# DeltaNet with an MLP: half of the batches with their token halves exchanged

## The chip, the cores and the metric

The kernel runs on one core of a Trainium2 chip. What is measured is the device time of one execution in microseconds (us), and what is compared is the median of several executions. One further execution is recorded by the hardware profiler; from it come the page of the profile and the trace.

A core has five engines that run side by side, each of them in its own program order: TensorE (PE in the profile) multiplies matrices, VectorE (DVE), ScalarE (ACT) and GpSimd (POOL) do elementwise work, and SyncE (SP) only issues transfers (DMAs). They meet at semaphores. PE's array of 128 by 128 can be used in smaller pieces, here called places: a matmul that contracts over at most 32 or 64 rows and writes 32 or 64 output partitions takes only the place at those rows and columns, and matmuls at other places can run beside it. The profile gives a place as rows*columns, `32*32` or `48*64` (48 rows lie in a place of 64).

## The reference

There are 4 batches of 8 heads, 768 tokens, and a head dimension of 48. Every (batch, head) pair carries a 48 by 48 state, and its tokens are a recurrence:

```python
k_n = k / (np.linalg.norm(k, axis=-1, keepdims=True) + 1e-06)
for t in range(S):
    y[:, :, t] = einsum('bhd,bhde->bhe', q_t, state)
    v_old = einsum('bhde,bhd->bhe', state, k_t)
    state = state + beta_t * einsum('bhd,bhe->bhde', k_t, v_t - v_old)
```

The heads of a token, side by side, make a row of 384 numbers. Of each row x the kernel then computes a LayerNorm without offset, two products with a ReLU between them (384 to 1536 and back to 384), and adds x: `x + relu(xn @ w_ch1) @ w_ch2`.

## The kernel before, in words

**Chunks.** The 768 tokens are 12 chunks of C = 64, and a chunk is two blocks of BK = 32 tokens. Within a chunk the recurrence is a triangular system. With the Gram matrix of the keys (the products of every pair of keys in the chunk) and the state S from the chunk before, a chunk needs these steps:

- `ks` = K S and `qs` = Q S, in `recur` (L886): what the old state answers to keys and queries. `ks` goes to the PSUM tile `two`, `qs` to the tile `by`. DVE then subtracts `ks` from v (L893).
- U, the solution of the triangular system, in three products (L908). The first multiplies v of one block by the inverse of that block's diagonal part (`xd`); ACT copies it to `u` (L914). The second multiplies it by the off-diagonal part of the Gram matrix (`goff`); DVE subtracts it from v of the other block (L912). The third multiplies that by the other block's inverse, and ACT copies again.
- the new state (L929, called s) and y = qs + P U (L919), where P holds the masked products of keys and queries (`pt`).

**Layout.** The 32 (batch, head) pairs are 2 pairs of batches (e) by 2 batches in a pair (g) by 8 heads; a head is j and a parity hp. A chunk of tokens of one pair of batches lies in one `half` of the partitions, 64 rows, and a block in one `quad`, 32 rows. The j index runs over 8 values, j = 0 to 3 for the batch g = 0 and j = 4 to 7 for g = 1. Each step loops over j and over the four (hp, e). In U a matmul reads 32 rows (a quad) and writes 32 partitions (a quad), and with (hp, e) alone the 64 matmuls of a product use four places.

**Gram.** For chunks up to 4, `gram` (L608 and what it calls) and `queries` (L643) make the Gram matrix and the key-query products apart. From chunk 5 on (JOINT), `gram_queries` (L666, its matmuls in L680) makes both: for each head and each of the two blocks one matmul at a place of 48*32, with 64 key columns and 64 query columns as moving data, 128 in all. For the second block the 32 columns that stand for the first block's tokens are not used afterwards. ACT copies the diagonal parts to `gdiag` (L691) and the off-diagonal ones to `goff`; DVE masks the key-query products into `pt`.

**Inverses.** `rows_inverse(m)` inverts the diagonal blocks of two chunks, 2m+1 and 2m+2, on DVE: a transposition of `gdiag` (L828), 31 pairs of row operations (L849, L856), and a transposition at the end (L861), which gives X(m) to U. Chunk 0 has a shorter way, `rows_near` and `near_join` (L807 to L819), and its U is called u0.

**Keys and queries.** `load_raw` and `load_v` load k and v with tokens on partitions (four DMAs and two DMAs for a chunk). `load_blocks` loads k or q once more in blocks, in eight DMAs, and `turned` (L577) transposes them on DVE; for chunks 0 to 3 PE transposes k instead (`first_kt`). The results stay in slots shared with other data: `kts`, `qts` and `pts` have four each, some in the same memory as the inverses' scratch tiles and `e_`, `d_` of the MLP.

**MLP.** The MLP of a chunk is 256 tokens. For chunks 0 to 2 the first product is plain (L1184, units of 6 matmuls); from chunk 3 on it is `fifteen` (L1100), 15 products of sub-blocks. The second product is plain for chunk 0 (L1206, pairs of matmuls), and `seven` (L1281), seven products in place of eight, from chunk 1 on. Sums and differences of sub-blocks are on GpSimd, DVE and ACT (L1267, L1113, L1306).

**Order.** `add` and `pe` only collect steps with what they read and write. `line.emit(ORDER)` then emits them as the list ORDER of step numbers has it, and `in_this_order` makes this each engine's program order, for DMA issues too. So the list alone decides where a small block of the recurrence stands between the matmuls of the MLP on PE. Before the first real work PE runs 26 steps of matmuls on zeros (`warm`, L1364), and three more (`fill`).

Of the kernel before, what the change touches and what calls it, by code (L numbers as in the profile page):

```python
# [16 lines left out]
C = 64  # L17
# [40 lines left out]
def pool(n):  # L58
# [161 lines left out]
def kernel(  # L220
# [16 lines left out]
    DM = H * D  # L237
    DFF = w_ch1.shape[1]
    KC = DM // 128
    FT = DFF // 128  # L240
    GH = 2 * H
    NP = H // 2
    TURNED = 4
    LNPE = 2
    GP = 2 * NP
    FROM = 3
    TOK = 256
    WN = 768

# [96 lines left out]
    def one_of(c):  # L346

        return c % 2 if c < 3 else (0, 0, 2, 3)[c - 3 if c < 4 else 1 + (c - 4) % 3]

    def kt_of(c):  # L350
        return c if c < 4 else (c - 4) % 3
# [513 lines left out]
    def xt_keys(c):  # L865
        return [("xd", slot(c))]
# [613 lines left out]
```

## Time and profile before

| | us |
|---|---|
| median of three runs | 512.43 (509.69 to 512.50) |
| the profiled execution | 510.23 |
| its span (first to last instruction) | 508.5 |
| granted clock, mean | 0.981 |
| PE busy | 486.6 (96% of the span) |
| DVE busy | 387.7 (76%) |
| POOL busy | 248.8 (49%) |
| ACT busy | 187.3 (37%) |
| L908, U products | x2304 matmuls of 0.201 each, many at a time |
| L680, joint Gram | x896 matmuls of 0.269 each |
| L886, ks and qs | x1344 matmuls of 0.218 each |
| issues on SP | 323 DMAs |

Busy time counts an engine as busy while any of its instructions runs, so it does not say how full PE's array is. In the lines of a timeline the columns are the start, the duration of the whole group in us, engine, source line, operation, output<-input, for a matmul the place and the tile, and the number of instructions. The duration of a group reaches to the end of its last instruction, which overlaps with the first of the next; what a block costs is read from one start to the next start. In the table of windows, each row is a stretch of the span, with the busy time of each engine and the number of its instructions (x), the clock granted to PE (1.00 is full), the share of time in which the DMA engines moved data, and GB/s.

### The profile page before, as it was taken

The numbers are of one execution on the slowest core, as the hardware profiler recorded it, in microseconds if no ns is written. First come the engines' busy times: TensorE is split into PE (matmuls) and PEld (weight loads), VectorE is DVE, ScalarE is ACT, GpSimd is POOL, SyncE is SP. The second block draws the span as 40 slices with busy tenths as digits, with TensorE's granted clock in tenths as the row PEclk, the third lists the DMA queues.
The fourth block names the chain that finished last, engine by engine and source line by source line (L and its number), as shares of the span: only waits on it lengthen the run. The fifth ranks groups of instructions, "written<-read, shape, count | busy, mean of one in ns | idle before, by whom it ended". The sixth has DMA issues, their size and how long they took to land.

```text
span 508.5 us, 21970 instructions
## 1 busy us (share of the span) xinstructions
PE 486.6 (96%) x9688; PEld 437.7 (86%) x9688; DVE 387.7 (76%) x855; ACT 187.3 (37%) x404; POOL 248.8 (49%) x377
## 2 busy tenths in 40 slices
PE   8668799999999999999999999999999999999996
PEld 5456686778898899999999989999999999999995
DVE  0865999989999967849999848999979889363241
ACT  2785544535512224442233433413431421424130
POOL 5036223302574588582291464492681671826553
PEclk9969799999999999999999999999999999999999
DMA  6986965532643332554234441520421303002011
GB/s 105 286 206 119 236 99 124 71 55 40 118 59 63 78 72 60 98 89 59 71 65 80 100 74 47 101 54 2 115 47 40 80 3 95 6 31 64 1 40 31
DMA packets 155855, 40.47 MB, mean 80 GB/s; under 512 B 149232, under 2 KB 152304, under 8 KB 155760
## 3 DMA queue, kind: packets, MB, share of 16 engines
q1 hardware_dynamic: 151920, 29.41, 31.7%
q10 hardware_dynamic: 3552, 9.63, 5.9%
q8 instruction: 76, 1.25, 1.0%
q14 instruction: 19, 0.16, 0.1%
q0 software_dynamic: 288, 0.03, 0.1%
HBM read 30.79 MB, written 8.26 MB: 77 GB/s over the span
## 4 chain that ended last, share of the span: by engine, by line
PE 82%; DVE 9%; issue 3%; DMA 2%; ACT 1%; POOL 1%; SPq 1%; DVEq 0%; POOLq 0%
PE f L1281 29%; PE f L1100 24%; PE f L1184 6%; PE two L908 5%; PE f L1206 3%; DVE tmp L849 3%; PE two L680 2%; PE by L886 2%; DVE xb L856 2%; PE two L886 2%; PE by L919 2%; PE f L1364 2%; PE two L929 1%; DVE kq L577 1%; DMA v<-in_v_dram 1%
## 5 line engine op out<-in xcount | busy, mean ns | idle before, releaser
L1267 POOL TENSOR_TENSOR h_all<-h_all 128x256 f32<-128x256 f32 x99 | 75.1, 770 | 14.9 <-ACT h_all L1193 11.4
L1281 PE MATMUL f<-w_sb,h_all 128*128 128x192 f32 x396 | 81.3, 331 | 0.0
L849 DVE TENSOR_TENSOR tmp<-xb,gb 128x31 f32<-128x31 f32 (+15 forms) x186 | 76.5, 411 | 4.7
L1281 PE MATMUL f<-words,h_all 128*128 128x192 f32 x396 | 77.7, 331 | 0.7 <-DVE o L1299 0.7
L856 DVE TENSOR_TENSOR xb<-xb,tmp 128x31 f32<-128x31 f32 (+15 forms) x186 | 72.5, 390 | 3.7
L1113 DVE TENSOR_TENSOR h_all<-f,h_all 128x512 f32<-128x512 f32 x90 | 60.6, 685 | 18.0 <-PE f L1100 17.5
L1306 POOL TENSOR_TENSOR words<-h_all 128x128 f32<-128x128 f32 x66 | 30.5, 482 | 83.0 <-ACT h_all L1116 51.7
L1281 PEld LDWEIGHTS f<-words,h_all 128*128 128x128 f32 x396 | 65.2, 190 | 2.5 <-DVE o L1299 0.8
L1281 PEld LDWEIGHTS f<-w_sb,h_all 128*128 128x128 f32 x396 | 64.6, 190 | 1.6 <-issue 0.4
L1184 PE MATMUL f<-xnt,w_sb 128*128 128x256 f32 x216 | 51.3, 386 | 0.6 <-DVE xnt L1012 0.6
L1108 ACT COPY h_all<-f 128x512 f32<-128x512 f32 x36 | 21.0, 585 | 73.0 <-PE f L1100 39.3
L1100 PE MATMUL f<-kt,w_sb 128*128 128x128 f32 x360 | 45.7, 276 | 0.0
L1184 PEld LDWEIGHTS f<-xnt,w_sb 128*128 128x128 f32 x216 | 39.8, 190 | 6.8 <-issue 0.9
L1116 ACT ACTIVATE h_all<-h_all 128x512 f32<-128x512 f32 x54 | 32.1, 624 | 34.4 <-DVE h_all L1113 34.3
L1100 PEld LDWEIGHTS f<-kt,w_sb 128*128 128x128 f32 x360 | 43.3, 192 | 0.4 <-issue 0.2
L914 ACT COPY u<-two 128x768 f32<-128x768 f32 x24 | 19.1, 797 | 47.9 <-PE two L908 41.7
L1100 PE MATMUL f<-xnt,w_sb 128*128 128x128 f32 x288 | 35.0, 276 | 0.0
L1100 PEld LDWEIGHTS f<-xnt,w_sb 128*128 128x128 f32 x288 | 33.3, 192 | 0.3
L1281 PE MATMUL f<-w_sb,words 128*128 128x192 f32 x132 | 28.1, 330 | 0.0
L1083 POOL TENSOR_TENSOR kt<-xnt,kt 128x128 f32<-128x128 f32 x9 | 4.1, 454 | 48.2 <-PE f L1100 48.2
L1193 ACT ACTIVATE h_all<-f 128x256 f32<-128x256 f32 x36 | 13.7, 384 | 36.8 <-PE f L1184 31.8
L532 POOL TENSOR_TENSOR w_sb<-words 128x768 uint32<-128x768 uint32 (+1 forms) x9 | 12.2, 1365 | 28.3 <-DVE words L519 22.5
(202 smaller groups left out, 886.6 us busy)
## 6 DMA issues: line engine op xcount, KB each, us to landing
words<-in_moe_w_ch_dram ACTq DMA_DIRECT2D x8, 768.0 KB, 7.0
v<-in_v_dram SPq DMA_DIRECT2D x24, 192.0 KB, 4.1
out_dram<-o SPq DMA_DIRECT2D x48, 96.0 KB, 2.4
kr<-in_k_dram SPq DMA_DIRECT2D x46, 96.0 KB, 3.3
xld<-xlt SPq DMA_DIRECT2D x9, 384.0 KB, 2.5
xnt<-xld SPq DMA_DIRECT2D x36, 96.0 KB, 2.8
tb<-in_q_dram SPq DMA_DIRECT2D x40, 64.0 KB, 3.0
tb<-in_k_dram SPq DMA_DIRECT2D x32, 64.0 KB, 2.9
```

Of the source, the lines that this page charges most:

```text
L849: lambda j=j, n=n, w=w, t=t: nc.vector.tensor_tensor(out=t, in0=xb[:, 0:n, j : j + 1].to_broadcast([128, n, w]), in1=gb[:, j : j + 1, j + ...
L856: "DVE", dve(n * w), lambda t=t, rest=rest: nc.vector.tensor_tensor(out=rest, in0=rest, in1=t, op=ALU.subtract),
L886: nc.tensor.matmul(dst[half(e), hp, j], src[drows(hp), (e if n else key_half(c, hp, e)) * GP + j], s_all[drows(hp), e, j], start=(n == 0 o ...
L908: nc.tensor.matmul(*args(e, e ^ hp, 2 * j + hp))
L1100: nc.tensor.matmul(wide(p[:, 128 * n : 128 * n + 128]), w[:, 128 * n : 128 * n + 128], r, start=start and n == 0, stop=True, skip_group_ch ...
L1108: add("ACT", act(512), lambda: nc.scalar.copy(to[0], ps(p)), pk, to[1])
L1113: add("DVE", dve(512), lambda: nc.vector.tensor_tensor(out=to[0], in0=in0, in1=in1, op=op), [*pk, *y[1]], to[1])
L1116: add("ACT", act(512), lambda: nc.scalar.activation(to[0], to[0], ACTF.Relu), [], to[1])
L1184: nc.tensor.matmul(p[:, 0:TOK], w1_sb[:, t, f * 128 : (f + 1) * 128], xnt[:, t], start=(t == 0), stop=(t == KC - 1))
L1267: add(eng, cost, lambda: e.tensor_tensor(out=out_, in0=x, in1=y, op=op), r, w, port=2 if eng == "Pool" else 1)
L1281: lambda f=f, t=start and f == 0: nc.tensor.matmul(p[:, 0:D2], lhs(f), rhs[:, f], start=t, stop=(f == F2 - 1), skip_group_check=True),
L1306: lambda f=f + i: e.tensor_tensor(out=s3[f], in0=one(0, 0)[0](f), in1=one(1, 0)[0](f), op=ALU.subtract),
```

## The change

From chunk 3 on (FIRST = 3), for the batches with g = 1 the two 32-token blocks of a chunk are stored exchanged: the tokens of block 1 lie in the quad where block 0 lies for g = 0, and the other way round. This holds for v, the raw keys, beta, the Gram matrix, the inverses, U and P; `ks` is written to exchanged quads.

- U: j alternates between the two batches, and the places of the one are not those of the other, so a product's 64 matmuls use eight places.
- `gram_queries` serves chunks 3 and 4 as well. The second block's matmuls leave out the 32 unused columns, so 128 and 64 columns alternate. The batches' halves are exchanged, so each place has the same number of columns in all. `goff` is one copy of 128 partitions for each half of the heads in place of two of 32; the key-query mask is an integer AND with a table, `pmask4`.
- `ks`: each matmul of a g = 1 head becomes two, of 32 output partitions each, 96 in place of 64 for a chunk. `qs` keeps its 64.
- Loads: `load_v` has six DMAs in place of two, `load_raw` twelve in place of four, beta more and smaller ones. SP issues 451 DMAs in place of 323, and the number of bytes stays.
- `gram` for chunks 1 and 2 has 64 matmuls of 64 columns in place of 128 matmuls, and four `gdiag` copies.
- Three slots for k, q and pt (`c % 3`); the inverses' scratch, `e_` and `d_` have memory of their own, and the waits that the sharing needed are gone.
- A new ORDER. `rows_inverse(0)` no longer waits for the whole load of beta, and part of its row operations stand ahead of the end of `near_join`. G3 and G4, the preparation of `rows_inverse(1)` and most of the MLP of chunk 0 stand behind u1 on PE, where before more of them stood ahead of it.

```diff
-    TURNED = 4
+    FIRST = 3
...
-    kts = [kq[:, 0] for kq in kqs] + [sb("kt3", [128, GH, C])]
-    qts = [kqs[0][:, 1], sb("qt1", [128, GH, C]), kqs[1][:, 1], kqs[2][:, 1]]
-    pts = [sb(f"pt{i}", [128, GH, C]) for i in range(2)] + [xn1, xt1]
+    kts, qts = [kq[:, 0] for kq in kqs], [kq[:, 1] for kq in kqs]
+    pts = [sb(f"pt{i}", [128, GH, C]) for i in range(3)]
...
     def kt_of(c):
-        return c if c < 4 else (c - 4) % 3
+        return c % 3
+
+    def other(j):
+        return j // NP
...
     def load_v(c, **kw):
         for e in range(2):
-            dma("SP", vs[c % NV][half(e)], nat(v, c, e), GH * C, 16.5, w=[("v", c % NV, e)], **kw)
...
+            dma("SP", to[half(e), 0], src[0, c * C : c * C + C], H * C, 16.5, w=keys[:1], **kw)
+            for b in range(2):
+                t0 = c * C + BK * (1 - b)
+                dma("SP", to[quad(2 * e + b), 1], src[1, t0 : t0 + BK], H * BK, 16.5, w=[keys[1 + b]], **kw)
...
-        def prod(g):
-            for j in range(NP):
+        def prod(x):
+            for i in range(NP):
+                g, j = i // 2, i % 2 + 2 * x
                 for hp, e in hp_e:
                     l = ((2 * e + g) * NP + j) * C
                     for b in range(2):
-                        f = l + b * BK
-                        both = kqs[ki].rearrange("p n h t -> p (n h t)")[drows(hp), f : f + 1]
-                        both = bass.AP(tensor=both.tensor, offset=both.offset, ap=[both.ap[0], [GH * C - b * BK, 2], [1, C]])
-                        nc.tensor.matmul(two[quad(2 * (e ^ hp) + b), hp, j * 2 * C : (j + 1) * 2 * C], flat[drows(hp), 0, f : f + BK], both)
+                        f, w = l + b * BK, C - b * BK
+                        k_ = flat[drows(hp), f : f + BK]
+                        both = bass.AP(tensor=k_.tensor, offset=k_.offset, ap=[k_.ap[0], [GH * C, 2], [1, w]])
+                        to = two[quad(2 * (e ^ hp) + (b ^ g)), hp, i * 2 * C : (i + 1) * 2 * C]
+                        to = bass.AP(tensor=to.tensor, offset=to.offset, ap=[to.ap[0], [C + b * BK, 2], [1, w]])
+                        nc.tensor.matmul(to, k_, both)
...
             def state(dst, src, n):
-                for j in range(GP):
+                js = range(GP) if c < FIRST or n else [g * NP + i for i in range(NP) for g in range(2)]
+                for j in js:
                     for hp, e in hp_e:
...
+                        w = src[drows(hp), (e if n else key_half(c, hp, e)) * GP + j]
+                        if n or c < FIRST or not other(j):
+                            todo = [(half(e), w)]
+                        else:
+                            todo = [(quad(2 * e + b), w[:, BK * (1 - b) : BK * (2 - b)]) for b in range(2)]
+                        for to, w in todo:
+                            nc.tensor.matmul(
+                                dst[to, hp, j], w, s_all[drows(hp), e, j], start=(n == 0 or j == 0), stop=(n == 0), skip_group_check=True,
+                            )
...
-            (0, lambda e, o, h: (p_2[quad(2 * o), h % 2, h // 2], xd[quad(2 * e), h], vv[quad(2 * e), h])),
+            (0, lambda e, o, h, x: (p_2[quad(2 * o + x), h % 2, h // 2], xd[quad(2 * e + x), h], vv[quad(2 * e + x), h])),
...
             def prod_u(args=args):
-                for j in range(GP):
+                for j in (g * NP + i for i in range(NP) for g in range(2)):
...
     recur(1)
+    prep_gq(3)
+    prep_gq(4)
     mlp(0)
     differences("DVE", dve(F2 * D2))
-    rows_inverse(1)
```

More of the change, by code (lines that the diff above doesn't have):

```diff
@@ L385 @@
         )
-    for i in (2, 1):
+    for i in (1,):
         c_dve(
@@ L427 @@
         )
+    c_pool(lambda: nc.gpsimd.memset(pmask4, 1.0), 0.5, ["pmask4"])
+    for n in range(4):
+        for x in range(2):
+            c_pool(
+                lambda n=n, x=x: nc.gpsimd.affine_select(
+                    out=pmask4[quad(n), 2 * x : 2 * x + 2], in_=pmask4[quad(n), 2 * x : 2 * x + 2], compare_op=ALU.is_gt, fill=0.0,
+                    base=-BK * (n % 2 ^ x), pattern=[[0, 2], [1, C]], channel_multiplier=-1,
+                ),
+                0.35, ["pmask4"],
+            )
+    c_dve(
+        lambda: nc.vector.tensor_scalar(
+            out=pmask4.bitcast(I32), in0=pmask4.bitcast(I32), scalar1=0, scalar2=-1, op0=ALU.is_gt, op1=ALU.mult
+        ),
+        0.4, ["pmask4"],
+    )
     c_dve(lambda: nc.vector.memset(eps, 1e-6), 0.06, ["eps"])
@@ L562, in scale_v @@
     def scale_v(c, kn, kk, **kw):
-        vk = [("v", c % NV, e) for e in range(2)]
+        vk = v_keys(c)
         add(
@@ new lines, in gram_near @@
+        for g in range(2):
+            pe(64, lambda g=g: prod((g,)), keys[g : g + 1], pk, 0.43, per=0.0097, **kw)
+        (nr, v, pk), = pair[4]
+        v = v.rearrange("p n (j t) -> p n j t", t=C)
+        for x in range(2):
+            o = gd16.rearrange("p t u (j n) -> p n j u t", n=2)[:, x]
+            v_ = v[:, x, :, 0:BK].rearrange("p j (u t) -> p j u t", u=2)
+            add("ACT", 0.62, lambda o=o, v=v_: nc.scalar.copy(o, v), pk, [("g16n", x)], **kw)
+        o = jn(GNAT)
+        add("ACT", act(512), lambda o=o, v=v: nc.scalar.copy(o, v[:, :, :, 0:BK]), pk, ["gn"], **kw)
@@ L722, in rows_near @@
         add(
-            "DVE", dve(512 * K), lambda: nc.vector.transpose(flat(gb, K * 512), gd), gdk + [("gdx", c, x) for c in chunks for x in range(2)],
+            "DVE", dve(512 * K), lambda: nc.vector.transpose(flat(gb, K * 512), gd), [("g16n", x) for x in range(2)],
             ["gb"], **kw,
@@ L1042, in sums_of_w1 @@
     def sums_of_w1(last):
-        gone = [(n, 1, *x) for n in ("qt", "pt") for x in ((), *((g,) for g in range(2)))]
         E = lambda i: (e_[i], [("E", i)])
@@ L1060, in sums_of_w1 @@
                 "Pool", 1.32, lambda o=o, a=a, b=b, op=op: nc.gpsimd.tensor_tensor(out=o, in0=a, in1=b, op=op),
-                [*ak, *bk, *([] if last else raw)], ok, after=[x for key in ok for x in pieces_(key)] if last else gone,
+                [*ak, *bk, *([] if last else raw)], ok, after=[x for key in ok for x in pieces_(key)] if last else ["gn", ("g16n", 0), ("g16n", 1), "xn", "es"],
             )
@@ L1068, in B @@
         def B(k, g):
-            return xnt[:, k].rearrange("p (i g b) -> p g i b", g=2, b=BK)[:, g], [("xnt", c % 2, x, k) for x in range(2)]
+            order = "p (g i b) -> p g i b" if c <= LNPE else "p (i g b) -> p g i b"
+            return xnt[:, k].rearrange(order, g=2, b=BK)[:, g], [("xnt", c % 2, x, k) for x in range(2)]
         def wide(t):
@@ L1083, in comb @@
                 "Pool", 0.47, lambda: nc.gpsimd.tensor_tensor(out=o, in0=x, in1=y, op=op), xk + yk, ok,
-                after=[("kt", 3, g) for g in range(2)],
             )
```

277 lines of the change are left out of this document (139 added, 138 removed), and 222 rows, old and new, of the table ORDER.

## The prediction

> **What bounds the kernel now.** I read the windows of busy time first, since the engines' shares of the page are averages over unlike stages.
>
> ```profile
> core 0: us, PE busy (x) PEld busy (x) DVE busy (x) ACT busy (x) POOL busy (x), PEclk, DMA share, GB/s
> 0.00:62.10 62.10, 47.18 (x1328) 34.30 (x1328) 37.64 (x111) 37.27 (x69) 22.25 (x37) 0.86 0.79 189
> 62.10:84.80 22.70, 22.14 (x334) 17.04 (x334) 21.53 (x48) 10.01 (x22) 6.75 (x6) 1.00 0.59 105
> 84.80:148.80 64.00, 63.35 (x1475) 50.76 (x1474) 59.78 (x125) 25.91 (x67) 25.55 (x29) 1.00 0.50 81
> 148.80:503.50 354.70, 353.96 (x6557) 335.64 (x6556) 268.37 (x573) 114.07 (x246) 194.29 (x309) 1.00 0.29 59
> ```
>
> From 62.1 us to 503.5 us TensorE (PE) idles for under 2 us, at a granted clock of 1.00. A saving outside PE is worth something only before that. In the head the bound is VectorE (DVE), read from its timeline:
>
> ```profile
> 40.07 0.72 DVE L819 COPY_PREDICATED xt<-mask,f 128x512 f32<-128x512 int32 x1 [2.16 <-PE f L812]
> ...
> 48.48 2.23 DVE L849 TENSOR_TENSOR tmp<-xb,gb 128x31 f32<-128x31 f32 x1
> ...
> 81.84 2.12 DVE L861 STREAM_TRANSPOSE xt<-xb 128x1024 f32<-128x1024 f32 x1
> ```
>
> The inverse for chunks 1 and 2 starts its row operations at 48.48, and its last transpose ends at 83.96; the first product of u1 (L908) starts at 84.78. From then on the time is a sum of PE blocks. Their costs start to start are read from PE's timeline:
>
> ```profile
> 326.66 1.06 PE L1100 MATMUL f<-xnt,w_sb 128*128 128x128 f32 x8
> 327.55 1.47 PE L1281 MATMUL f<-w_sb,h_all 128*128 128x192 f32 x8
> 328.94 0.88 PE L908 MATMUL two<-v,xt 32*32 32x48 f32 x64
> 329.76 0.92 PE L1281 MATMUL f<-w_sb,h_all 128*128 128x192 f32 x4
> ```
>
> ```profile
> 360.41 1.15 PE L886 MATMUL two<-s_all,kq 48*64 48x48 f32 x64
> 361.38 1.11 PE L886 MATMUL by<-s_all,kq 48*64 48x48 f32 x64
> 362.42 1.24 PE L1281 MATMUL f<-w_sb,h_all 128*128 128x192 f32 x6
> ```
>
> ```profile
> 301.31 1.16 PE L680 MATMUL two<-kq 48*32 48x128 f32 x64
> 302.39 1.15 PE L919 MATMUL by<-u,pt 64*64 64x48 f32 x64
> ```
>
> So a U product costs 0.82 (329.76−328.94), a ks or qs block about 1.0 to 1.08, a Gram block (G) 1.08. Block costs times counts from u1 on: MLP 317.3, U 26.9, G and P (queries) 18.6, ks 10.8, qs 10.5, y 11.6, s 8.5, together 404.1. A visit of PE from the MLP's 128-row matmuls to a small block and back costs 0.197 more; 71 visits make 14.0. The sum, 418.1, meets the measured 503.5−84.78 = 418.7, so PE is never short of work there and every term below counts in full.
>
> **U products.** In the single records four matmuls start 6.7 ns apart, and the fifth waits until 42.5 ns after the first: only four places, each taken for one 48-column stream. 15 such rounds and the last three starts make 0.68, and 0.13 passes until the next block. With eight places eight records issue in 54 ns, longer than 42.5, so issue binds: 64×6.7 = 0.43, plus 0.13 = 0.56. The densest other stream, L812's 128 small records, shows 8 to 8.5 ns each, which gives 0.67. I take 0.60. The 27 products of chunks 3 to 11 save 27×0.215 = **5.8**.
>
> **Gram.** L680 already shows eight starts 6.7 ns apart, then a wait to 110 ns for 128 columns. The mean now is 96 columns, the same total at every place: eight rounds of 83 ns (0.667) less the last, plus the 0.2 that L680 leaves to its successor and the slower first round, about 0.83; bounds 0.78 and 1.09 (nothing gained). 18 joint blocks stand behind u1 where before there were 14, with two P blocks more and the wide G4; G and P together go from 18.6 to 16.0, **−2.6**.
>
> **ks.** Here the change costs. For nine chunks the block goes from 64 to 96 records, since each 64-wide place of the g=1 heads becomes two of 32; and as j alternates between g=0 and g=1, the place size alternates: eight segments. The trace has 150 changes of place size behind 62 us, and at each one the first matmul starts 70 ns before the previous one *ends* (131 to 149 ns after its start); between L929 and L919, both 64×64, nothing is lost. After a change L886's first round takes 254 ns a record instead of 218. A segment of four records is then 20+254−70 = 0.204, one of eight 47+228−70 = 0.205 (228: the 201 to 204 ns of a 48-column record plus the 24 that first rounds of L908 and L680 show). Four pairs make 1.63. Lower bound 1.05 (96 records with no such wait), upper 2.02 (whole 0.25 per segment). I take 1.63, since all changes of this trace agree: 9×0.55 = **+5.0**.
>
> The Trainium skill, "TensorEngine Tiling (Array Packing)", Key Properties, says that changing the tiling mode drains TensorE while changing only the tile does not. That speaks against this change; the 70 ns before the end, at every change, agree with it, though no run here changes size inside a block of such short segments.
>
> **Head.** rows_inverse(0) no longer waits behind the load of beta, part of its row operations are put ahead of L819, and other DVE work (weight words, a 1.25 transpose L577, the 1.22 of L838) leaves the stretch. Adding durations by form in DVE's order, L819 to the end of X(0) was 41.8 (in 43.9 of time) and becomes 32.0. From 40.07, with half of the 2.1 idle and the 0.82 to PE, u1 starts at **74.0** instead of 84.8. Bounds: 70.8 (the 2.16 wait at L819 gone too) and 78.5 (all the idle, 1.3 of DVE work moved ahead of L819, and the 3.5 by which row operations of 2.23, 1.20 and 0.78 exceeded their form's usual 0.2 to 0.4 this time).
>
> But what PE did under that cover comes later. Behind u1 stand 33 instead of 26 first-product units of the MLP (1.29 each) and seven more second-product pairs (0.68): 9.0+4.8 = **+13.8**. That is the answer to the early u1.
>
> **The rest** I cost at nothing. 128 more SP issues at 0.53 to 0.69 make 77 us of SP, but SP waits for buffers of the previous chunks for far longer in all, and a load stands ahead of its use by tens of us; without that cover a late v or k would hold ks or s. The issues of v and k are also queued past stores of o, which nothing on PE reads. One 128×512 ACT copy (0.585) in place of two 32-partition ones (0.366 each), the mask on DVE, the builder of pmask4 on GpSimd and the gdiag copies lie beside PE; by the same adding DVE finishes its work before PE needs it by 4 us at u3 and by over 20 later, where before X(1) was level with u3. Three slots take waits away that PE did not show.
>
> **Sum.** From u1: 418.1 + 13.8 − 5.8 − 2.6 + 5.0, and three visits fewer (−0.6): 427.9. Span: 74.0 + 427.9 + 0.7 idle + 5.0 tail = 507.6, against 508.5. The profiled execution took 1.73 more than its span (510.23), and the median is 2.20 above it; so I add 3.9: **511.5** against 512.43.
>
> **Rivals.**
> *No stop inside ks.* If matmuls of two sizes follow each other inside a block as on free places, ks stays at 1.05 to 1.08, 5.0 less: span 502.6, **506.5**. For it: narrow records of L608 start ahead of wide ones, so the array's places are not one queue. Against: the 150 changes.
> *Slower: the head gives nothing back.* The moved 13.8 is paid for certain, the 10.8 of u1 only if DVE's chain is as dense as added. If the chain to X(0) ends where it did (held by another load, or by row operations that GpSimd slows, as the 2.23 may be), the span is 84.8+427.9+5.7 = 518.4, **522.3**. It decides beyond u1 = 80 us (+1%). For it: 2 us of idle and the long row operations in this very stretch. Against: the row operations need only gb, ready before.
> *The eight places do nothing.* If a place is released only in issue order, or issue is the floor, U stays at 0.815 and G at 1.09: 5.8 and 4.7 more than forecast, **522**. For it: the late half of L680 starts at 16 ns per record. Against: 6.7 ns within every round.
>
> The Trainium skill, "TensorE: Matmul & The Clock Gate", Part 1 ("Wait — 56ns, not 53.3ns?"), states that matmul starts are never closer than about 25 ns. By it a U product's 64 records would take 1.6 us on eight places as on four, and the change would gain nothing there. The 6.7 ns of L908 and L680 on separate places, and the 0.68 of L908's 64 records, speak against it.
>
> **How the numbers follow.** Chances: forecast 0.50, no stop 0.24, head 0.17, places 0.09. Within 1% (about what this kernel's measurement can tell from no change) is 507.3 to 517.6. No stop lies at its lower edge, two thirds of it count as faster (0.16), with the forecast's early end (u1 near 71, U at 0.56) 0.09: 0.25. Slower: head 0.13, places 0.08, the forecast's late end (u1 past 78, ks at 2.0) 0.07: 0.28. Same 0.47. The forecast's own range is 505 to 517; the range that leaves out 2 in 10 is 503 to 522.5: below it only no stop with an early u1, above it the outer ends of the two slow cases.
>
> **What would show it.** U blocks at 0.55 to 0.67 start to start, joint Gram at 0.83, ks at 1.6 in eight segments with about 0.2 from one segment's first start to the next; the first U product of u1 at 71 to 78; PE idle below 3 us behind it. A ks block of 1.1, u1 at 85, or PE idle on a DMA of v or kr would prove me wrong.

## The result, and the profile after

The changed kernel takes **528.87 us** (median of 526.05 to 530.65) against 512.46 for the kernel before: a ratio of 1.0327, with a 95% interval of 1.026 to 1.0395. The forecast was 511.5, and its range ended at 522.5. The profiled execution of the changed kernel has a span of 529.0 us against 508.5.

The windows of busy time of the changed kernel, read as those of before:

```profile
core 0: us, PE busy (x) PEld busy (x) DVE busy (x) ACT busy (x) POOL busy (x), PEclk, DMA share, GB/s
0.00:73.00 73.00, 56.44 (x1214) 43.00 (x1215) 51.40 (x152) 43.85 (x75) 23.09 (x45) 0.77 0.73 171
73.00:84.80 11.80, 10.29 (x404) 8.36 (x404) 6.87 (x11) 4.72 (x10) 8.71 (x8) 1.00 0.38 50
84.80:95.00 10.20, 8.09 (x137) 6.13 (x140) 6.37 (x8) 3.75 (x11) 7.92 (x7) 0.83 0.41 58
95.00:148.80 53.80, 50.90 (x1113) 37.81 (x1101) 48.19 (x102) 21.20 (x56) 13.63 (x13) 1.00 0.49 87
148.80:524.00 375.20, 372.91 (x6882) 350.38 (x6874) 273.63 (x586) 114.34 (x247) 197.15 (x317) 1.00 0.29 58
```

In the kernel before, PE was short of work for under 1 us from 84.80 to 148.80 (63.35 of 64.00 busy). Now it is idle for 1.5, 2.1 and 2.9 us in the three stretches up to 148.80 and for 2.3 us in the next, and in one of them the granted clock is 0.83. The first product of u1 (now L972) starts at 72.97:

```profile
72.97 0.88 PE L972 MATMUL two<-v,xd 32*32 32x48 f32 x64
...
388.17 0.80 PE L972 MATMUL two<-v,xd 32*32 32x48 f32 x64
388.90 0.43 PE L1344 MATMUL f<-words,h_all 128*128 128x192 f32 x1
```

These are two groups of PE's timeline. The product at 72.97 belongs to chunk 1 and uses four places; the one at 388.17, of chunk 9, uses eight and costs 0.73 from its start to the next. The joint Gram (L734) and ks (L942) in the same timeline:

```profile
286.43 1.14 PE L734 MATMUL two<-kq 48*32 48x128 f32 x64
287.50 0.49 PE L1163 MATMUL f<-d_all,e_all 128*128 128x128 f32 x2
```

```profile
380.74 2.10 PE L942 MATMUL two<-s_all,kq 48*64 48x48 f32 x96
382.77 0.43 PE L1344 MATMUL f<-w_sb,h_all 128*128 128x192 f32 x1
```

Gram costs 1.07 where it cost 1.09, ks 2.03 where it cost 1.08. Behind u1 everything on PE, from start to next start, adds up like this (us; waits are counted with the step ahead of them; the two measured sums hold 0.5 more for the last matmul, and the forecast's is its 427.9 with its 0.7 of idle time):

| | before | after | as forecast |
|---|---|---|---|
| u1 starts at | 84.8 | 73.0 | 74.0 |
| MLP, plain products (L1247, L1269) | 47.8 | 67.1 | 61.6 |
| MLP, fifteen and seven | 282.0 | 282.5 | 282.0 |
| ks | 10.6 | 19.3 | 15.6 |
| U | 26.8 | 26.3 | 21.0 |
| Gram and P | 18.5 | 21.0 | 15.9 |
| qs, state, y, turns of xn | 32.5 | 34.2 | 32.5 |
| from u1 to PE's end | 418.7 | 450.9 | 428.6 |

So u1 gains 11.8, and the stretch behind it grows by 32.2. The difference is the 20.5 us of the span. Of the 22.3 us by which that stretch missed the forecast, the block sizes make 11.5: nine ks blocks at 2.03 instead of 1.63 are 3.6, 27 U products at 0.732 instead of 0.60 are 3.6, and 18 Gram blocks at 1.07 instead of 0.83 are 4.3. The other 10.8 are mostly waits of PE and matmuls at a lowered clock: the gaps between PE's records are 8.7 us in sum, where the prediction had 0.7. They sit in the plain products (5.5), in U (1.7), in the last row of blocks (1.7) and in Gram (0.8).

One of these waits, on PE's timeline and on DVE's, and the windows around it:

```profile
83.54 1.14 PE L734 MATMUL two<-kq 48*32 48x128 f32 x64
84.61 0.91 PE L1269 MATMUL f<-w_sb,h_all 128*128 128x384 f32 x2
85.36 1.46 PE L1247 MATMUL f<-xnt,w_sb 128*128 128x256 f32 x6
88.93 1.76 PE L734 MATMUL two<-kq 48*32 48x128 f32 x64 [2.11 <-DVE pt L748]
90.62 3.73 PE L1247 MATMUL f<-xnt,w_sb 128*128 128x256 f32 x12
```

```profile
85.74 1.25 DVE L615 STREAM_TRANSPOSE kq<-tb 128x1024 f32<-128x1024 f32 x1 [1.42 <-DMA tb<-in_q_dram]
86.91 1.13 DVE L441 TENSOR_SCALAR pmask<-pmask 128x256 int32<-128x256 int32 x1
88.18 0.69 DVE L748 TENSOR_TENSOR pt<-two,pmask 128x512 int32<-128x512 int32 x1
```

```profile
87.00:89.00 2.00, 0.07 (x8) 0.07 (x15) 1.86 (x4) 0.42 (x2) 2.00 (x2) 1.00 0.29 34
89.00:91.00 2.00, 2.00 (x65) 1.64 (x66) 1.35 (x2) 0.00 (x0) 2.00 (x3) 0.50 0.64 91
91.00:93.00 2.00, 2.00 (x7) 1.61 (x7) 1.90 (x3) 1.50 (x4) 1.72 (x2) 0.64 0.48 70
93.00:95.00 2.00, 2.00 (x60) 1.56 (x62) 0.00 (x0) 0.01 (x1) 0.00 (x0) 1.00 0.65 88
```

The first half of Gram 3 ends at 84.7. Its results leave `two` only when DVE masks them (L748). In DVE's order that stands behind a transposition that waits for the DMAs of chunk 4's q, and behind the building of pmask4 (L441). The second half of Gram 3, in the same tile, starts at 88.93. PE stood for 2.1 us, and the next 4 us ran at a granted clock of 0.50 and 0.64: two MLP units of about 1.4 us each took 3.7. The wait alone does not bring the lower clock. In u_four, one of the kernels below, which up to here differs only in the order of heads within U, PE stood at this place for 2.5 us, the clock stayed at 1.00, and the two units took 2.8 us:

```profile
88.68 1.14 PE L734 MATMUL two<-kq 48*32 48x128 f32 x64 [2.50 <-DVE pt L748]
89.75 2.86 PE L1247 MATMUL f<-xnt,w_sb 128*128 128x256 f32 x12
```

```profile
89.00:91.00 2.00, 2.00 (x62) 1.68 (x42) 1.93 (x4) 0.39 (x1) 2.00 (x3) 1.00 0.62 94
```

### The profile page after: what moved, and what is told of

Its sections match the earlier page's. It is cut to its first block, busy times and chain, and to the rows that moved or that the text cites. A ratio compares the mean times of both kernels' runs of the same rounds, so it can differ in the third digit from the quotient of the medians.

```text
span 529.0 us, 22174 instructions
## 1 busy us (share of the span) xinstructions
PE 498.6 (94%) x9712; PEld 445.7 (84%) x9712; DVE 386.8 (73%) x858; ACT 187.9 (36%) x398; POOL 250.6 (47%) x387
## 4 chain that ended last, share of the span: by engine, by line
PE 72%; DVE 10%; SPq 6%; issue 3%; DMA 3%; ACT 3%; POOL 1%; POOLq 0%; DVEq 0%; ACTq 0%
PE f L1344 27%; PE f L1163 22%; SPq L375 6%; PE f L1247 5%; PE two L972 4%; PE two L942 3%; PE two L734 3%; DVE tmp L901 3%; DVE xb L908 2%; PE by L942 2%; PE by L983 2%; DMA words<-in_moe_w_ch_dram 1%; PE two L993 1%; POOL h_all L1330 1%; PE f L582 1%
## 5 line engine op out<-in xcount | busy, mean ns | idle before, releaser
L1330 POOL TENSOR_TENSOR h_all<-h_all 128x256 f32<-128x256 f32 x99 | 73.7, 755 | 19.6 <-ACT h_all L1256 8.7
L901 DVE TENSOR_TENSOR tmp<-xb,gb 128x31 f32<-128x31 f32 (+15 forms) x186 | 74.2, 399 | 4.0
L1369 POOL TENSOR_TENSOR words<-h_all 128x128 f32<-128x128 f32 x66 | 32.7, 513 | 50.7 <-ACT h_all L1179 40.0
L1247 PE MATMUL f<-xnt,w_sb 128*128 128x256 f32 x216 | 54.1, 397 | 0.0
L1163 PE MATMUL f<-d_all,e_all 128*128 128x128 f32 x360 | 47.6, 277 | 0.0
L1247 PEld LDWEIGHTS f<-xnt,w_sb 128*128 128x128 f32 x216 | 41.0, 197 | 7.8 <-ACT h_all L1256 0.6
L1163 PE MATMUL f<-d_all,w_sb 128*128 128x128 f32 x360 | 46.1, 276 | 0.0
L978 ACT COPY u<-two 128x768 f32<-128x768 f32 x24 | 19.2, 798 | 75.4 <-PE two L972 66.3
L1163 PEld LDWEIGHTS f<-d_all,e_all 128*128 128x128 f32 x360 | 44.7, 191 | 0.7 <-ACT h_all L1171 0.2
L1163 PEld LDWEIGHTS f<-d_all,w_sb 128*128 128x128 f32 x360 | 43.4, 192 | 0.4 <-issue 0.2
L1179 ACT ACTIVATE h_all<-h_all 128x512 f32<-128x512 f32 x54 | 31.7, 624 | 27.9 <-DVE h_all L1176 27.7
L1163 PEld LDWEIGHTS f<-xnt,w_sb 128*128 128x128 f32 x288 | 33.8, 192 | 0.4 <-DVE h_all L1176 0.2
L1362 DVE TENSOR_TENSOR o<-f,x 128x192 f32<-128x192 f32 x33 | 11.4, 349 | 27.9 <-PE f L1344 24.7
L1362 POOL TENSOR_TENSOR o<-o,words 128x192 f32<-128x192 f32 x22 | 14.2, 649 | 36.9 <-DVE words L1362 33.4
```

Source lines behind the costliest of these rows:

```text
L901: lambda j=j, n=n, w=w, t=t: nc.vector.tensor_tensor(out=t, in0=xb[:, 0:n, j : j + 1].to_broadcast([128, n, w]), in1=gb[:, j : j + 1, j + ...
L1163: nc.tensor.matmul(wide(p[:, 128 * n : 128 * n + 128]), w[:, 128 * n : 128 * n + 128], r, start=start and n == 0, stop=True, skip_group_ch ...
L1179: add("ACT", act(512), lambda: nc.scalar.activation(to[0], to[0], ACTF.Relu), [], to[1])
L1247: nc.tensor.matmul(p[:, 0:TOK], w1_sb[:, t, f * 128 : (f + 1) * 128], xnt[:, t], start=(t == 0), stop=(t == KC - 1))
L1330: add(eng, cost, lambda: e.tensor_tensor(out=out_, in0=x, in1=y, op=op), r, w, port=2 if eng == "Pool" else 1)
L1362: lambda: e.tensor_tensor(out=out_, in0=a, in1=b_, op=ALU.add), r, w,
```

## Experiments

In the table, "before" is the kernel before, run on the same chip beside the other, and the last two columns come from the profiled execution.

| kernel | us | before | ratio (95%) | u1 at | from u1 |
|---|---|---|---|---|---|
| changed | 528.87 | 512.46 | 1.0327 (1.026 to 1.0395) | 73.0 | 450.9 |
| ks_grouped | 522.41 | 511.43 | 1.0227 (1.0173 to 1.028) | 72.8 | 442.3 |
| gram_alternate | 527.28 | 511.43 | 1.0308 (1.0268 to 1.0347) | 71.2 | 449.1 |
| loads_whole | 527.23 | 511.43 | 1.0305 (1.0266 to 1.0343) | 73.2 | 448.6 |
| no_exchange | 524.87 | 511.43 | 1.0259 (1.022 to 1.0297) | 73.0 | 446.3 |
| u_half_columns | 526.79 | 511.11 | 1.0301 (1.0252 to 1.0351) | 72.3 | 447.9 |
| u_four | 528.69 | 510.30 | 1.0347 (1.0297 to 1.0397) | 72.7 | 450.4 |
| order_moved | 531.46 | 511.11 | 1.0388 (1.0348 to 1.0427) | 72.5 | 454.4 |
| order_ks_gram | 525.48 | 511.11 | 1.0262 (1.0213 to 1.0312) | 72.1 | 447.6 |
| q_two_buffers | 527.35 | 510.30 | 1.0341 (1.03 to 1.0382) | 73.2 | 448.6 |
| few_loads | 524.50 | 510.30 | 1.0282 (1.0252 to 1.0312) | 71.9 | 446.7 |
| few_moved | 528.60 | 510.30 | 1.0363 (1.0329 to 1.0396) | 72.5 | 448.5 |
| rows_short | 521.87 | 510.41 | 1.0207 (1.0157 to 1.0258) | 69.6 | 444.0 |
| rows_short_few | 521.55 | 510.41 | 1.021 (1.0159 to 1.0261) | 72.8 | 442.1 |
| ks_gram | 520.33 | 510.41 | 1.0177 (1.0122 to 1.0232) | 72.0 | 441.9 |

u1 differs by up to 3.4 us between kernels that are the same up to there (rows_short and changed). So where a verdict turns on a few us, I read the stretch from u1 on, and the blocks themselves. Two limits go with that. The kernel before took 510.3 to 512.5 in these rounds, so a difference between two times of the table is good to about 2 us; steadier is how far each time lies above the kernel before beside it, 16.4 us for the changed kernel. And a stretch is one execution's: that of the changed kernel holds a wait of 1.55 us at 235.9 (PE for ACT, L1179), and with it 84.1 us from u4 to u6, where loads_whole, q_two_buffers, few_loads and rows_short take 82.2. Those 1.9 us are no effect of what these four change near u1.

### ks: what a change of place size costs inside a block

```diff
-                js = range(GP) if c < FIRST or n else [g * NP + i for i in range(NP) for g in range(2)]
+                js = range(GP)
```

> The changed kernel with one edit: ks takes all j of g = 0 and then all of g = 1, so the place size changes once in the block instead of seven times. In the changed kernel a ks block takes 2.03 us. Theory: the stops at each change of place size make that. Then the block is eight rounds of 64-wide records (0.61 to the next size) and 64 records of 32 (0.63 to 0.75), 1.25 to 1.35 us; nine blocks save 6 to 7 us, the time is about 522. Rival: the 32 further records are the cost, whatever their order; then the block stays at 1.9 to 2.0 us and the time at 528 to 529.

It came as the theory has it: 522.41, 6.5 us less than the changed kernel (5.4 when each is set against the kernel before beside it), and a ks block of 1.35 us, which makes 6.1 in nine blocks (PE's timeline of ks_grouped):

```profile
373.99 1.42 PE L942 MATMUL two<-s_all,kq 48*64 48x48 f32 x96
375.34 0.92 PE L1344 MATMUL f<-w_sb,h_all 128*128 128x192 f32 x4
```

The 96 records are the same; only their order differs. The starts of one alternating ks block of the changed kernel (chunk 9, the first two of eight segments, ns to the next start, from the trace's single records) show what each change costs:

```
64-wide, 8 records:   7   6   7  73   7   7   6 | 149
32-wide, 16 records:  6   7   7   6   7   7   6  20   7   7   6   7   7   6   9 | 132
```

After the last record of a segment the next size starts 149 or 132 ns later, 70 ns before that record ends, as at the block boundaries of the kernel before. A segment of eight takes 0.262 us, one of sixteen 0.247, and four pairs 2.03. The Trainium skill, "TensorEngine Tiling (Array Packing)", Key Properties, has the rule that a change of tiling mode drains TensorE; here the trace agrees, to within those 70 ns, in segments of 0.25 us too.

### U and Gram: what binds at eight places

```diff
-                        nc.tensor.matmul(*args(e, e ^ hp, 2 * j + hp, x_(j)))
+                        o_, l_, r_ = args(e, e ^ hp, 2 * j + hp, x_(j))
+                        nc.tensor.matmul(o_[:, 0 : D // 2], l_, r_[:, 0 : D // 2])
```

> The changed kernel, where every matmul of U streams 24 instead of 48 columns; the other 24 columns of U are left out. In the changed kernel a U block takes 0.73 us: the first 32 records start 7 ns apart with a pause after each eight, then about 0.1 us passes, and the rest start every 8.5 ns. Theory: the rate at which records reach PE binds the second half, whatever they stream; then the first 32 are quicker by under 0.1, and the block stays at 0.64 to 0.73. Rival: the places are still busy with columns; then the block falls to 0.45 to 0.55, and 33 products save 6 to 9 us.

With half of the columns a U product still takes 0.67 us (PE's timeline of u_half_columns):

```profile
384.98 0.74 PE L973 MATMUL two<-v,xd 32*32 32x24 f32 x64
385.65 0.59 PE L1345 MATMUL f<-words,h_all 128*128 128x192 f32 x2
```

So at eight places the columns make no more than 0.06 us of the block; the rate at which the records come binds. With 24 columns four places do as well: chunks 1 and 2 also take 0.67, where with 48 columns they take 0.81. In the changed kernel, the starts of a U block (chunk 9, all 64 records summed by parts): the first 32 start within 199 ns, 6.4 ns apart; then come gaps of 54 and 42 ns; the last 30 gaps make 306 ns, 10.2 each. With 24 columns the late records come two by two, every 17 ns. L680 in the kernel before showed the same turn after 32 records. Each record has a weight load ahead of it (PEld in the profile), and the loads show the turn too: in this U block 99 ns pass behind the 32nd load, and then two come about every 17 ns. Whether the loads set this rate or something ahead of both, no run here tells apart: 24 columns leave the loads as they are.

```diff
-                for j in (g * NP + i for i in range(NP) for g in range(2)):
+                for j in range(GP):
```

> The changed kernel, where a U product takes j in the order 0 to 7, so first all of g = 0 at four places and then all of g = 1 at the other four. Within the kernel before such a product took 0.81 us, with alternation it takes 0.73. If four places at a time bind, the block goes back to 0.78 to 0.81, 27 products add 1.3 to 2.2 us, 530 to 531; if the supply of records binds alone, it stays at 0.73 and the time at 529.

The block goes to 0.787 (386.88 to 387.67), not quite to 0.81. The time, 528.69, can't tell 1.5 us; the block can. The eight places are worth 0.055 to 0.08 us a product.

```diff
-            for i in range(NP):
+            for i in (0, 2, 1, 3):
                 g, j = i // 2, i % 2 + 2 * x
```

> The changed kernel with one edit: in the joint Gram block the heads are issued in the order g = 0, 1, 0, 1 instead of 0, 0, 1, 1, so that each place gets 128 and 64 columns in turn. The block takes 1.07 us in the changed kernel. Theory: two long streams in a row at half of the places hold up the records behind them; alternating gives 0.85 to 0.9 us, 18 blocks save 3 to 4 us, the time is about 525.5. Rival: the supply of records binds (in the single records the first 32 start close together, the later ones every 8 to 16 ns); then the block stays at 1.0 to 1.1 and the time within 1 us of 528.9.

Nearer to the rival: the block falls to 0.985 (317.50 to 318.49 in PE's timeline below), 18 of them by 1.5 us, and the time by 1.6 (0.6 against the kernel before). The order of long and short streams at a place held 0.085 us of the block. The greater part, down to 0.83, did not come.

```profile
317.50 1.06 PE L734 MATMUL two<-kq 48*32 48x128 f32 x64
318.49 0.71 PE L1163 MATMUL f<-d_all,w_sb 128*128 128x128 f32 x4
```

### The exchange and the order apart

In no_exchange all parts of the exchange are undone, the order stays.

```diff
     def other(j):
-        return j // NP
+        return 0
...
-                        to = two[quad(2 * (e ^ hp) + (b ^ g)), hp, i * 2 * C : (i + 1) * 2 * C]
+                        to = two[quad(2 * (e ^ hp) + b), hp, i * 2 * C : (i + 1) * 2 * C]
```

> The changed kernel without the exchange: loads in one piece, ks with 64 records at 64-wide places, U at four places, Gram with 128 and 64 columns but each place with always the same; the new order, the slots and the early inverse stay. By the block costs: ks 9 x 0.95 less, U 27 x 0.08 more, Gram as it is. If the idle time on PE comes from SP, 5 to 8 us go too, and the time is 514 to 518; if it comes from the order, the time is 521 to 523. In both it stays above the kernel before (512.5), since 13.8 us of the MLP stand behind u1.

It took 524.87, above both expectations. The blocks did as expected, 1.08 for ks, 0.81 for U and 1.07 for Gram; with their waits ks adds up to 10.5 again, U to 29.4, Gram to 21.8. The 8.8 us saved at ks are partly lost again at U. Most of all: without any exchange the new order, with the slots and the early inverse, is 13.4 us slower than the kernel before. So the larger half of the loss is the order, not the places.

### What PE waits for behind u1

In loads_whole v, raw k and beta are loaded in one piece.

```diff
-            dma("SP", to[half(e), 0], src[0, c * C : c * C + C], H * C, 16.5, w=keys[:1], **kw)
-            for b in range(2):
-                t0 = c * C + BK * (1 - b)
-                dma("SP", to[quad(2 * e + b), 1], src[1, t0 : t0 + BK], H * BK, 16.5, w=[keys[1 + b]], **kw)
+            together("SP", vs[c % NV][half(e)], nat(v, c, e), GH * C, 16.5, keys, **kw)
```

> The changed kernel with v, raw k and the later part of beta loaded in one piece for both batches, as in the kernel before (v 2 DMAs a chunk, k 4, beta 8 for 16), each issued where the last of its parts stood: 116 issues fewer on SP. The tokens of g = 1 are then not exchanged, which leaves that part of the computation out; all other work is as in the changed kernel. Theory: PE's 8.7 us of idle time between u1 and u6 comes from SP, which issues without a pause from 63 to 117 us; then 5 to 8 us of it go, the time is 521 to 524. Rival: it comes from the new order, whose chains through ACT and DVE have nothing of the MLP beside them; then the time changes by less than 1.5 us.

The time fell by 1.6 us, just above the rival's bound, and by 0.6 against the kernel before; PE's gaps fall from 8.7 to 5.7 us, 1.6 of it the wait at 235.9. So 116 issues fewer on SP are worth little. The expectation had also misread SP: in the changed kernel it issues nothing from 70.9 to 73.7, 82.5 to 87.0, 95.8 to 98.9 and 102.1 to 105.1 us, so it is not the rate of issues that fills this stretch.

In order_moved eight steps stand elsewhere in ORDER, among them (numbers of the steps):

```diff
 DVE
-  476 (transposes k or q of chunk 4), 26 (pmask4), 451 (mask of Gram 3, first half)
+  26, 451, 476
 PE
-  u1, y1, s1, 568 (MLP unit)
+  u1, 568, y1, s1
-  Gram 3 second half, 582, 572 (MLP units)
+  572, Gram 3 second half, 582
-  ks3, 680 (MLP unit)
+  680, ks3
```

> The changed kernel with eight steps moved in its order, nothing else: on DVE the mask of chunk 3's first half of P goes ahead of the transposition of chunk 4's q that waits for its DMAs; on PE units of the MLP that were ready go ahead of y1, of the second half of G3, of u2, of G5 and of ks3, and G8 ahead of a unit of the MLP that waits for ACT. Theory: the order leaves PE without ready work there, for 7 us, and the 2.1 us of idle before the second half of G3 is followed by 4 us at a granted clock of 0.50 and 0.64; both go, 6 to 9 us less, 520 to 523. Rival: the work is short anyway, and the idle time comes back at the next small block; then less than 2 us.

My theory failed here: 531.46, slower than the changed kernel. The wait of 2.1 us ahead of Gram 3's second half is gone, but two of 1.2 and 0.9 us stand ahead of its first half and of Gram 4's, and one of 5.2 us came up behind them:

```profile
97.11 2.10 PE L1269 MATMUL f<-w_sb,h_all 128*128 128x384 f32 x6
104.36 2.93 PE L1247 MATMUL f<-xnt,w_sb 128*128 128x256 f32 x6 [5.15 <-ACT h_all L1256]
```

```profile
100.28 1.25 DVE L615 STREAM_TRANSPOSE kq<-tb 128x1024 f32<-128x1024 f32 x1 [6.45 <-DMA kr<-in_k_dram]
```

These are PE's and DVE's timelines of order_moved. The MLP units that had been moved ahead were missing here, while DVE stood at a transposition that waits for the loads of chunk 2's q (the transposition reads `tb`, and the semaphores it waits for are those of q's loads; the profile names a load of raw k that came last on one of them). From 94 to 97 us the DMA engines were busy throughout, at 326 GB/s, with two loads of the MLP's weights, 768 KB each, issued at 91.92 and 94.17; whether these held q's loads up was not tried.

> The moved order, with the Gram heads in turn and ks grouped, the 32-wide places first, so that the 64-wide half stands next to qs of the same size. Grouping gave 6.5 us, the Gram turn 1.6, the order should give 6 to 9, and the half next to qs up to 0.9: if they add up, 512 to 515, level with the kernel before or up to 0.7% above it. If the idle time only moves, 518 to 521.

525.48 says the same: with the moved order the two repairs of blocks end 5.2 us above what they reach without it (ks_gram, below; 4.5 against the kernel before).

Then three kernels eased the loads or took some away. In q_two_buffers q of chunk 4 has its own buffer:

```diff
-        load_blocks(1, q, c, "SP")
-        turned(c, 1, qts[kt_of(c)], ("qt", kt_of(c)))
+        qb = 3 if c == 4 else 1
+        load_blocks(qb, q, c, "SP")
+        turned(c, qb, qts[kt_of(c)], ("qt", kt_of(c)))
         gram_queries(c)
```

> The changed kernel, but the q of chunk 4 is loaded to a buffer of its own (the memory of the MLP's differences, not yet in use) instead of tb1, through which the q of chunks 3, 4 and 2 go one after the other between 57 and 107 us; the order is the same. Theory: this one buffer makes DVE, and PE behind it, wait before the second half of G3 and before the queries of chunk 2; then 2 to 5 us less, 524 to 527. Rival: the rate of issues on SP (0.5 us each, without a pause from 63 to 82 us) makes the wait, or the order; then less than 1.5 us.

The time, 527.35, and its ratio of 1.0341 show no gain. From u1 on it is 2.3 us shorter, but 0.4 of that lies between u1 and u3, where the buffer is used, and 1.9 between u4 and u6.

In few_loads the second half of each block load goes too:

```diff
-                    dma(
+                    (none if u else dma)(
                         eng, dst[p0 : p0 + BK, :, u, 0:w],
```

> The changed kernel with as few loads as I can give it: v, raw k and beta in one piece, the q of chunk 4 in its own buffer, and of the block loads of q and k only the first 32 tokens of each chunk (the second half, and the exchange of the batches, are left out of the computation). Everything on PE, DVE, ACT and GpSimd is as in the changed kernel. Theory that loads hold the head: PE's idle time behind u1, 8.7 us, falls under 3 and the half-clock stretch goes, 519 to 522. Theory of the order: waits for ACT and DVE remain without a load in them, 5 us or more of idle, 525 to 527 (the loads in one piece alone gave 527.2).

> The same few loads with the eight steps moved, which alone made the time 531.5, since PE ran out of ready work at 99 us and stood for 5.2 us until the q of chunk 2 had come. If loads were what spoiled the moved order, it now gives what was hoped of it: idle under 2.5 us behind u1 and 517 to 520, below few_loads. If the work itself is short there (the chain of inverse, mask and layer norm on DVE), idle stays above 4 us and the time is no lower than that of few_loads.

With few loads the stretch from u1 on is 4.2 us shorter (446.7), 1.8 of it between u1 and u3, and PE's gaps above 0.25 us fall from 8.7 to 3.8 us in sum, but the time is 524.5: short of the loads theory, at the edge of the other. The moved order stays worse also with few loads (528.60, 7.3 us of gaps), so the loads were not what spoiled it. Both runs point to DVE: in few_loads it is busy for 18.16 of the 20 us from 110 to 130 and 18.54 of the next 20.

In rows_short the second inverse leaves out half of its row operations:

```diff
+            if m == 1 and j % 2:
+                for _ in range(2):
+                    add("DVE", 0.0, lambda: None, ["gb"], ["xb"], **kw)
+                continue
```

> The changed kernel, where the second inverse (chunks 3 and 4) leaves out every second of its 31 pairs of row operations, some 11 us of DVE work between u1 and u3; that part of the computation is left out. Theory: DVE's work there makes the small blocks late, since masks, v and the layer norm stand behind row operations in its order; then PE's idle time behind u1 (8.7 us) halves or better and the time falls by 4 to 7 us, to 522 to 525. Rival: the waits are those for loads and for single results, whatever DVE has to do; then less than 2 us.

> The same short inverse with the few loads of few_loads. By the measured blocks (ks 2.03, U 0.73, Gram 1.07, the MLP without stalls) the stretch from u1 on is 439.6 us without idle time, and u1 stands at 72 to 73: a span of 518, a time of 518 to 520. If DVE and the loads together make the idle time, that is the result. If it stays above 522, there is a third cause in the order.

The windows of rows_short:

```profile
84.80:95.00 10.20, 10.20 (x198) 7.63 (x189) 6.74 (x9) 5.19 (x15) 4.67 (x4) 1.00 0.79 166
95.00:110.00 15.00, 15.00 (x222) 9.99 (x225) 12.55 (x28) 6.22 (x14) 4.16 (x3) 1.00 0.56 98
110.00:130.00 20.00, 19.76 (x531) 15.65 (x520) 14.89 (x27) 7.29 (x18) 4.67 (x4) 1.00 0.44 73
130.00:148.80 18.80, 18.04 (x533) 14.74 (x531) 13.90 (x20) 5.36 (x15) 8.68 (x11) 1.00 0.29 45
```

From 84.8 to 148.8 PE is idle for 1.0 us instead of 5.0, at full clock throughout. (Everything stands 3.4 us earlier here, so the wait ahead of Gram 3's second half, 1.33 us, lies just in front of these windows; from u1 on the gaps above 0.25 us are 2.9 us instead of 8.7.) The time is 521.87, 11.5 us above the kernel before in place of 16.4, so 5.0 less. The stretch from u1 on is 6.9 us shorter, 444.0; of these 5.5 lie between u1 and u3, where the second inverse is worked on, and 1.9 between u4 and u6.

So the stretch from u1 to u3 is what tells the causes apart. It takes 71.8 us in the changed kernel, 71.2 to 72.2 in gram_alternate, u_four, loads_whole and q_two_buffers, 69.9 with few loads, 66.3 with the short inverse, and 65.1 with both. DVE's row operations for the second inverse are worth about 5 us of PE's time there, the loads 1 to 2.

rows_short_few is at 442.1 from u1 on, 8.8 us less than the changed kernel, and the measured blocks without waits make about 439.6 (an estimate from the block costs). Of the 11.3 us between, 6.6 are DVE's row operations and the loads together, 1.9 are the stretch from u4 to u6, and 2.8 are not named by any run. The time, 521.55, lies between the 520 expected at most and the 522 beyond which a third cause was to be sought.

### The two repairs together

```diff
-                js = range(GP) if c < FIRST or n else [g * NP + i for i in range(NP) for g in range(2)]
+                js = range(GP) if c < FIRST or n else [*range(NP, GP), *range(NP)]
...
-            for i in range(NP):
+            for i in (0, 2, 1, 3):
                 g, j = i // 2, i % 2 + 2 * x
```

> The changed kernel in its own order, with ks grouped (the 32-wide places first, so that its 64-wide half stands next to qs) and the Gram heads in turn. Grouping alone gave 6.5 us, the turn 1.6; next to qs a change of size in nine blocks may save up to 0.09 each. If they add up, 519.5 to 521; that is still above the kernel before, since 13.8 us of the MLP stand behind u1.

520.33, as expected: the repairs add up, and standing next to qs gives little (ks is at 1.35 as in ks_grouped, but for the two with qs right behind, 1.24 and 1.29). It is the best version of the exchange tried here, and 1.8% slower than the kernel before.

## Why the prediction was wrong

Four terms failed, all to the slow side: the idle time of PE (10.8 us with the lower clock), Gram (4.3), ks (3.6) and U (3.6). Each rival of the prediction let one term fail at a time, so none of them reached 528.9.

**The early u1** was right, in the time and in the mechanism: 73.0 against 74.0. DVE's chain to the first inverse was as dense as added, 33.5 us from L819 (now L871) to the end of X(0) where the forecast has 33.0, and started 2.1 us earlier, at 37.95; what follows it took 0.7 longer. The MLP that stands behind u1 in exchange came as counted: 13.8 us of units stand there, more than the 11.8 that u1 gains, and the plain products grew by 19.3, the waits included.

**ks** failed in the length of a segment. The step said "a segment of four records". Each matmul of the source is two records in the trace (64 records for 8 values of j and four (hp, e)), so a segment has eight records, or sixteen; the step's own count of 96 records in eight segments asks for that too. The rule, 70 ns before the end and a slow first round, was right (the 131 to 149 ns from start to start stand behind 48-column records only; behind the MLP's they are 205 and more, and the 70 ns hold there too); with eight and sixteen it gives 0.26 and 0.25 a segment and 2.03 a block, which is the upper bound of the step (2.02). It is 3.6 us.

**U** failed in the rate. "64×6.7" held for the first 32 records only; 0.60 was taken near the fast end, though L812 with its 8 to 8.5 ns was the row of a long stream and the nearer one. 0.732 lies even above the bound of 0.67, which is what 24 columns give; with 48, the late records come 10.2 ns apart. It is 3.6 us.

**Gram** failed in "eight rounds of 83 ns": the mean of 128 and 64 columns is not what a round takes when a place gets its long streams one after the other and its neighbours wait. Alternating brought 0.985, and the supply of records the rest, by the single records: argued for Gram, shown for U. It is 4.3 us.

**"PE is never short of work"** is the step that cost most. It was carried over from the kernel before, on the ground that DVE's added durations ended 4 us ahead of PE at u3. They did not: X(1), the second inverse, ends at 144.50 on DVE and u3 starts at 144.74 on PE:

```profile
142.40 2.10 DVE L913 STREAM_TRANSPOSE xd<-xb 128x1024 f32<-128x1024 f32 x1
```

```profile
144.74 0.80 PE L972 MATMUL two<-v,xd 32*32 32x48 f32 x64
```

The sum left out that DVE itself waits, for loads at L615 and for results of PE ahead of L748 ("a load stands ahead of its use by tens of us" failed here: the eight loads of chunk 4's q were issued from 73.7 to 82.5 us, and L615 stood until 85.74), and that masks and v for PE stand between the row operations in its order. Of the 10.8 us, 6.6 went when half of these row operations and part of the loads were left out, 5.5 with the row operations alone; 1.9 sit between u4 and u6 in this one execution; the rest is not named. A part is the clock: the 2.1 us ahead of Gram 3's second half were followed by matmuls that took 1.5 us longer at the lower clock, which the same wait in u_four did not bring.

**The rivals.** The slow one in the head had the wrong place: u1 came early and the kernel is slower all the same. That nothing stops inside ks is refuted. That the places do nothing came nearest for Gram, and for U the truth lies nearer to nothing (0.732 of 0.815) than to the forecast. The Trainium skill's floor of about 25 ns between matmul starts, "TensorE: Matmul & The Clock Gate", Part 1, did not appear on separate places: 10.2 ns is the mean of the slow half in U. But there is a rate that binds, and the prediction's own rows, L680 and L812, show it.

Of the 16.4 us by which the changed kernel is slower, the new order with its waits makes about 13.4 (no_exchange against the kernel before), the exchange on top of it 3.0 (4.6 by the two stretches from u1 on): ks costs 8.8 there, and U (3.1) and Gram (0.8), both with their waits, and smaller shifts take the rest back.

## What to carry to other kernels

Price a stream of small matmuls by a row as long as itself: here 32 records came at 6.4 ns and the rest at 8.5 to 10, and neither more places nor fewer columns brought a block of 64 under 0.67 us. Inside a block keep all places of one size together; each change costs what a block boundary costs, and grouping gave back 6.1 of ks's 8.7 us without any other edit. When work is moved behind an early start on the engine that bounds, it is not hidden but only moved; and a sum of durations on another engine says nothing on waits unless its own waits are in the sum. Two executions can differ by some us in places that an edit does not touch, so place a difference on the timeline before naming its cause.

## What was not expected of the hardware

After 32 records of a block of small matmuls the rate of starts drops: in U from 6.4 ns, with a gap of some 0.1 us between, to 10.2 ns (8.5 with half of the columns), and the turn stays close to that record. The weight loads turn with it. Idle time of PE can cost more than itself: 2.1 us were followed by 2 us at a granted clock of 0.50 and 2 us at 0.64. But its length does not decide: 2.5 us in u_four and 2.1 us at 230.9 us in ks_gram were followed by a clock of 1.00, and 1.06 us at 112.0 in gram_alternate by 0.57 from 114 to 118 us; what decides stays open. And the profiled start of u1 was 69.6 us in rows_short and 73.0 in the changed kernel, which are the same up to there, with a granted clock from 62.1 to 73.0 us of 1.00 in the one and 0.70 in the other; which of the two causes the other was not tried.
